# A fused attention and feed-forward kernel: a new order of all steps, with w_in's second quarter loaded ahead of batch 1's x

## The chip, the cores and the metric

The kernel runs on one core of a Trainium2 chip. The core has five instruction queues that run side by side, each strictly in its own order: TensorE (PE in the profile; its weight loads are PEld), VectorE (DVE), ScalarE (ACT), GpSimd (POOL) and SyncE (SP). SP computes nothing and issues DMAs; POOL computes and issues DMAs too. An instruction that waits for another engine holds up all that stands behind it in its queue. The metric is the device time of one execution in microseconds (us). Three runs of the kernel before took 211.12, 211.23 and 211.58 us; the median is 211.23 us.

## The reference: what is computed

There are 8 batches of 8 heads. Each head has 512 tokens and 32 states of width 64.

```python
scores = scale * x @ state.T                 # tokens read states
xread  = softmax(scores) @ state
scores2 = scale * state @ x.T                # states read tokens
sread  = softmax(scores2) @ x
y = concat([xread, sread])                   # 544 rows a batch, 8 x 64 wide
h = y @ w_in                                 # 512 -> 2048
g = maximum(h, 0) + alpha * minimum(h, 0)
out = g @ w_out                              # 2048 -> 512
```

Inputs and output are float32; the matrix work is done in float16.

## The kernel before

Nothing is scheduled by a tool at build time. The string ORDER holds 1115 short tokens, one a step, and the last loop of the kernel calls the step of each token in turn. A token is a name, its numbers (mostly batch first), sometimes an engine letter (a = ACT, v = DVE, p = POOL) and, where the step opens a PSUM bank, the number of the bank (0 to 5; one more tile of two banks, "two", is shared by scores and state projections). The place of a token fixes the place of its instructions in the queue of its engine, and so which instruction waits behind which. Waits between engines follow from the tiles.

**The attention part of a batch b.** `lx.b` (L161, POOL issues a casting DMA) loads x; three x buffers take turns, so `lx.b` must wait until the state reads `rd.(b-3)` have read the old one. `xd.b` (L291, SP) writes the transposed copy xT by a transposing DMA; batches 0 and 1 are transposed on PE instead (`xt` L299, copied out by `xo` L304). `sc.b` (L314, PE) makes the scores in the tile "two". From there two softmax chains go out. Over states: `sb` (L346, DVE), `smax` (L379, DVE), `ssh` (L384, POOL), `sexp` (L393, ACT), `ssum` (L400, L401, DVE), `snorm` (L404, DVE), `wb` (L412, DVE), whose result aT is the attention weight of every token. Over tokens: `tm` (L424, DVE), `nb` (L431 on ACT or L433 on DVE), `te` (L441, ACT), `tsum` (L451), `tn` (L457 ACT or L459 POOL), `tt` (L463, SP, a transposing DMA into e2T), then `rd` (L475, PE) and `rdo` (L486), the reads of the states. Batch 0 runs with half tiles and its own scores (`tsc`, L353), and its weights are turned on PE (`at`, `ao`).

**The feed-forward part.** xread is never made: `m.b.f` (L521, PE) multiplies the states by quarter f of w_in, `mo` (L545, L547) copies the product out, and the first layer `F.b.jc` (L570, PE, 16 blocks a batch) multiplies it by the weights aT. `N` (L623, ACT) takes the negative part, `G` (L626, DVE) builds g. In batch 0 four pairs of halves (`f`, `n`, `g`; L592, L607, L611) do the same for the first blocks. `F.8` is the block of all state reads.

The second layer of batch 0 is plain: `S.0.q.k` (L640, PE) adds two blocks of g against w_out, 8 such steps for each of 4 row quarters, `O` (L657, ACT) copies out. Batches 1 to 8 use seven products instead of eight: `U` (L707, POOL or DVE) makes sums of g, `W` (L683, POOL) sums of w_out once, `P.b.p.i.c` (L728, PE, four matmuls) are the products, `K` (L744) keeps a partial bank and `Q` (L759, L761) combines and sends out through SP. The four quarters of w_in (`wi`, L207) and of w_out (`wo`, L213) and the other states (`lst`, L201) come through POOL's DMA queue, one after another in the order of the tokens. `Z.k.n` are n dummy matmuls on bank k (L232); six more stand at the very start.

ORDER is written out in full in the file; no planner runs with the kernel, and no costs or due times are in it. What sets the work around the change is only the order of tokens on each queue, the six banks and "two", and the counts of buffers (three for x, two for xT, four for output tiles).

Of the kernel before, what the change touches and what calls it, by code (L numbers as in the profile page):

```python
# [32 lines left out]
m.2.2.5.3 mo.2.2.a.1 rdo.0.a sb.2 tn.1.1.p mo.2.2.a.0 F.1.3.1 tm.2 S.0.3.0.2 W.4.1.p F.1.0.3 N.1.0 smax.2 N.1.3 G.1.3
S.0.3.4 F.1.13.0 N.1.13 S.0.0.5 nb.2.a te.2.1 S.0.3.2 ssh.p.2 G.1.0 U.1.3.0.p F.1.7.5 N.1.7 te.2.0 G.1.7 tsum.2
S.0.3.6 S.0.3.5 S.0.3.7 F.1.14.1 N.1.14 G.1.13 S.0.3.3 G.1.14 tn.2.0.p tt.1 U.1.1.1.p U.1.2.1.p xd.3 sexp.2 S.0.0.2
m.2.3.3.5 m.4.3 mo.2.3.a.0 ssum.2.0 mo.2.3.a.1 S.0.0.0 F.1.9.1 N.1.9 mo.4.3.a G.1.9 S.0.3.1 S.0.0.6 O.0.3.a snorm.v.2
P.1.2.0.1.3 F.1.11.5 N.1.11 G.1.11 wb.2 m.3.2 mo.3.2.a S.0.0.7 F.1.10.1 N.1.10 G.1.10 S.0.0.4 O.0.0.a rd.1.2 rdo.1.a
# [775 lines left out]
```

## Time and profile before

| what | value |
|---|---|
| three runs | 211.12, 211.23, 211.58 us |
| profiled execution, its own time | 210.96 us |
| its span, first to last instruction | 209.2 us |
| PE busy | 199.0 us, 2024 matmuls |
| DVE busy | 182.0 us, 273 compute instructions and 2 memsets |
| POOL busy | 165.6 us |
| ACT busy | 150.9 us |
| granted TensorE clock | 1.000 |
| DMA | 23.71 MB, 113 GB/s in the mean |

The profiled execution stands 0.27 us below the median of the runs. A PE that is called busy is not always at its peak, since the ends of matmuls are modelled: the start times of one group and the next tell more than the busy share. POOL's spans are rough. In a timeline a row holds the start, the length, the engine, the line, the operation, the tile written and the tiles read, the shape and the count; a bracket behind it tells how long the engine stood idle and what ended it. In the chain of waits, equal neighbours are merged.

### The profile page before, as it was taken

How to read it: one execution, taken by the hardware profiler on the slowest of the kernel's cores; microseconds unless marked ns; L12 is line 12 of the kernel's file. 1: busy time of each engine (PE TensorE's matmuls, PEld its weight loads, DVE VectorE, ACT ScalarE, POOL GpSimd, SP SyncE). 2: the span in 40 equal slices, each digit the busy share in tenths (PEclk: the TensorE clock that was granted, in tenths of full speed). 3: DMA queues.
4: the chain of work that ended last, by engine and by line, in shares of the span. 5: the costliest groups of instructions: out<-in, count | busy, mean ns of one | idle time of the engine just before them, and what ended most of it. 6: DMA issues, size and time to landing. Idle time of an engine off the chain costs nothing.

```text
span 209.2 us, 5108 instructions
## 1 busy us (share of the span) xinstructions
PE 199.0 (95%) x2024; PEld 132.9 (64%) x2024; DVE 182.0 (87%) x275; ACT 150.9 (72%) x293; POOL 165.6 (79%) x105
## 2 busy tenths in 40 slices
...
GB/s 167 219 204 206 206 188 130 154 156 161 120 104 147 125 93 194 68 90 168 141 109 39 104 165 97 12 93 127 75 3 53 50 50 53 0 50 103 60 150 95
DMA packets 49992, 23.71 MB, mean 113 GB/s; under 512 B 34480, under 2 KB 49456, under 8 KB 49968
## 3 DMA queue, kind: packets, MB, share of 16 engines
...
## 4 chain that ended last, share of the span: by engine, by line
PE 61%; DMA 12%; DVE 11%; POOL 11%; issue 1%; ACT 0%; SPq 0%; POOLq 0%; DVEq 0%
PE px L728 19%; PE h L570 16%; PE pv L728 9%; POOL gsum L707 7%; DVE g L626 6%; PE py L728 6%; DMA w_in_sb<-in_moe_w_in_dram 5%; DMA st<-in_state_dram 4%; PE h L579 3%; PE o L640 2%; PE m_ps L521 2%; DMA xT<-xg 2%; DMA e2T<-e 2%; DVE oq L761 1%; DVE nb L424 1%
## 5 line engine op out<-in xcount | busy, mean ns | idle before, releaser
L626 DVE SCALAR_TENSOR_TENSOR g<-neg,oma_sb,h 128x512 f16<-128x512 f32 (+1 forms) x140 | 92.3, 707 | 7.4 <-ACT neg L623 6.8
L623 ACT ACTIVATE neg<-h 128x512 f32<-128x512 f32 (+1 forms) x140 | 75.1, 579 | 20.6 <-PE h L570 15.5
L570 PE MATMUL h<-aT,m 128*128 128x512 f16 x248 | 67.3, 379 | 0.2
L728 PEld LDWEIGHTS <-gsum 128*128 128x128 f16 x480 | 46.2, 98 | 13.0 <-issue 1.5
L728 PEld LDWEIGHTS <-g 128*128 128x128 f16 x360 | 35.1, 98 | 11.2 <-issue 0.9
L707 POOL TENSOR_TENSOR gsum<-g,g 128x1024 f16<-128x1024 f16 (+1 forms) x14 | 27.8, 1990 | 11.6 <-DVE g L626 7.2
L707 POOL TENSOR_TENSOR gsum<-gsum,g 128x1024 f16<-128x1024 f16 (+1 forms) x15 | 30.0, 2003 | 8.3 <-DVE gsum L707 7.5
L570 PEld LDWEIGHTS <-m 128*128 128x128 f16 x248 | 23.8, 98 | 16.1 <-issue 1.9
L728 PE MATMUL px<-ws,gsum 128*128 128x256 f16 x240 | 32.8, 273 | 0.0
L707 POOL TENSOR_TENSOR gsum<-g 128x1024 f16<-128x1024 f16 (+1 forms) x14 | 28.8, 2064 | 0.8 <-PE pv L728 0.8
L707 POOL TENSOR_TENSOR gsum<-g,gsum 128x1024 f16<-128x1024 f16 x12 | 25.4, 2130 | 0.2
L744 ACT COPY kept<-px 128x512 f32<-128x512 f32 (+1 forms) x20 | 11.5, 577 | 11.3 <-PE px L728 9.5
L547 ACT CAST m<-m_ps 128x512 f16<-128x512 f32 x33 | 18.0, 604 | 1.9 <-PE m_ps L521 1.7
L640 PE MATMUL o<-w_out_sb,g 128*128 128x512 f16 x64 | 17.5, 380 | 1.8 <-DVE g L626 1.0
L384 POOL TENSOR_TENSOR ts<-ts,mx 128x1024 f32<-128x1024 f32 x7 | 13.4, 1913 | 5.9 <-DVE mx L379 5.9
L728 PE MATMUL py<-w_out_sb,g 128*128 128x256 f16 x120 | 17.5, 273 | 0.1
L728 PE MATMUL px<-w_out_sb,g 128*128 128x256 f16 x120 | 16.7, 272 | 0.1
L728 PE MATMUL px<-w_out_sb,gsum 128*128 128x256 f16 x120 | 16.7, 273 | 0.0
L728 PE MATMUL pv<-ws,gsum 128*128 128x256 f16 x120 | 16.1, 273 | 0.0
L728 PE MATMUL pv<-ws,g 128*128 128x256 f16 x120 | 15.7, 273 | 0.0
L761 DVE TENSOR_TENSOR oq<-pv,kept 128x512 f32<-128x512 f32 (+1 forms) x16 | 10.4, 652 | 5.2 <-PE pv L728 4.8
L521 PE MATMUL m_ps<-w_in_sb,stT 64*32 64x512 f16 x256 | 12.6, 384 | 1.1 <-DMA w_in_sb<-in_moe_w_in_dram 0.4
...
## 6 DMA issues: line engine op xcount, KB each, us to landing
...
```

The costliest lines, as they stand in the source:

```text
L384: engine(e).tensor_tensor(blocks(cols(live["ts", b], j, S)), blocks(scored(b, j)), over_blocks(cols(live["mx", b], j, S // N)), ALU.subtract,)
L521: nc.tensor.matmul(t[N * k : N * (k + 1), :], st_head(b, h)[64 * r : 64 * r + 64, :], w_in_sb[64 * r : 64 * r + 64, c, 512 * f : 512 * (f ...
L547: copier(e)(m_tile(b, f)[:, g, :], t[g])
L570: nc.tensor.matmul(h.rearrange("p (r j s) -> p r j s", r=2, j=2), ms[b, f][:, g, 128 * j : 128 * (j + 1)], weights(b, g), start=(g == 0), ...
L579: nc.tensor.matmul(h, w_in_sb[:, c, 128 * jc : 128 * (jc + 1)], XS[:, c].rearrange("p q n b -> p (q n b)"), start=(c == 0), stop=(c == n_c ...
L623: nc.scalar.activation(neg, h, RELU, bias=0.0, scale=-1.0)
L626: nc.vector.scalar_tensor_tensor(g_tile(b, jc), negs.pop((b, jc)), oma_sb[:, jc : jc + 1], hs.pop((b, jc)), ALU.mult, ALU.add,)
L640: nc.tensor.matmul(outs[b, q], g_tile(b, jc)[:, 128 * q : 128 * (q + 1)], w_out_sb[:, jc, :], start=not begun and jc == 2 * jc2, stop=left ...
L707: engine(e).tensor_tensor(t, x(), y(), op)
L728: nc.tensor.matmul(pbanks[b, name][:, i, :], of(b, c)[:, j, 128 * i : 128 * (i + 1)], moving[:, 4 * c + j, :], start=not begun and j == 0, ...
L744: copier(e)(t, pbanks[b, "x"])
L761: nc.vector.tensor_tensor(osb, pbanks[b, name], kept[b, add], ALU.add)
```

## The change

Only ORDER differs. It has 1115 tokens before and after; no step is added or taken away, and several steps change their engine or their bank. The diff touches nearly every line of the string. The first lines of both, and later lines which hold steps that the text below names, are these:

```diff
--- before.py
+++ after.py
...
-Z.1.1 Z.2.1 stc.a cx.0.0.a stt.3 wi.0 sbd.0.a Z.4.1 cx.0.1.v xt.0.0.1.5 xo.0.0.1.a sbd.1.v xt.0.0.0.0 xo.0.0.0.v
-tsc.0.1.1 lst cx.1.0.a lx.1 sto.a cx.1.1.v tsc.0.0 Z.2.1 wi.1 smax.0.0 xt.0.1.1.4 xo.0.1.1.v xt.0.1.0.5 wo.0 tsc.1.1.0
-xo.0.1.0.a tsc.1.0 Z.2.1 m.0.0.3.4 ssh.v.0.0 sc.0.1 sexp.0.0 oma wi.2 mo.0.0.a.0 mo.0.0.a.1 Z.5.1 smax.0.1 ssum.0.0
-snorm.p.0.0 ssh.v.0.1 str.0.1 sro.0.a sc.0.0 tm.0 Z.2.1 sexp.0.1 str.1.5 Z.3.1 at.0.4 ao.0.v nb.0.v ssum.0.1
-xt.1.1.1.2 xo.1.1.1.v sro.1.a m.4.0.0.1 mo.4.0.v.0 te.0.1 te.0.0 xt.1.1.0.3 xo.1.1.0.a xt.1.0.1.4 f.0.1.0.5 mo.4.0.v.1
-m.1.0 mo.1.0.v f.0.0.0.2 n.0.1.0 snorm.p.0.1 xt.1.0.0.0 at.1.1 ao.1.v n.0.0.0 xo.1.0.1.a g.0.1.0.0 g.0.0.0.1 m.0.1.3.1
-xo.1.0.0.a sc.1 m.2.0.4.0 mo.0.1.a.1 mo.0.1.a.0 mo.2.0.a.0 g.0.0.0.0 S.0.2.0.1 mo.2.0.a.1 tm.1 sb.1 F.0.5.2 F.0.4.3
-nb.1.a wo.1 g.0.1.0.1 wi.3 f.0.1.1.4 N.0.5 G.0.5 F.0.6.0 te.1.0 smax.1 N.0.4 S.0.2.1 G.0.4 F.0.7.5 te.1.1 f.0.0.1.2
-m.0.2 N.0.6 n.0.1.1 G.0.6 g.0.1.1.1 mo.0.2.a g.0.1.1.0 wo.2 wo.3 tsum.0 S.0.1.2.3 S.0.2.2 F.0.11.0 N.0.7 G.0.7 ssh.p.1
...
-F.1.15.3 F.1.2.2 G.1.8 S.0.2.6 N.1.15 G.1.15 W.2.1.p S.0.0.3.4 N.1.2 S.0.0.1 rd.0.0 lx.3 tn.1.0.a sc.2 O.0.2.a G.1.2
...
-m.3.0.0.5 mo.3.0.a.1 lx.4 xd.4 sc.3 tm.3 P.1.2.1.1 mo.3.0.a.0 sb.3 F.2.9.4 N.2.9 G.2.9 nb.3.a F.2.11.2 F.2.10.5
...
-U.1.4.0.p P.1.3.1.0 W.4.0.p U.2.1.0.p P.1.3.0.0 m.4.1.5.1 mo.4.1.a.1 nb.4.v mo.4.1.a.0 rd.2.4 rd.3.3 P.1.4.0.1 F.2.7.1
...
-G.3.5 F.3.7.4 tn.4.0.p tt.4 N.3.7 G.3.7 P.2.3.0.0 F.3.14.0 N.3.14 F.3.3.2 N.3.3 P.2.3.0.1 lx.6 G.3.8 F.3.0.3 N.3.0
-F.4.1.4 N.4.1 P.2.3.1.0 te.5.1 G.3.14 F.4.5.5 P.2.3.1.1 Q.2.0.1.a U.2.3.0.p G.3.0 sb.5 P.2.7.1.0.0 G.3.3 N.4.5 te.5.0
...
-P.3.1.1.0 P.3.1.0.0 K.3.1.a m.5.3.2.3 sc.6 sb.6 smax.6 ssh.p.6 m.6.3.1.5 mo.6.3.a.1 P.3.6.0.1 mo.5.3.a.1 mo.6.3.a.0
...
-U.4.2.0.p P.3.7.1.0 P.3.7.1.1 K.3.4.a P.3.7.0.0 F.5.0.5 N.5.0 F.5.7.3 Q.3.1.1 F.5.4.1 N.5.7 N.5.4 tm.6 nb.6.v te.6.1
...
-nb.7.v P.4.4.1.1 P.4.3.1.0 te.7.0 G.6.0 U.5.1.0.p te.7.1 P.4.4.0.0 N.6.13 P.4.3.0.0 G.6.1 G.6.4 tsum.7 tn.7.0.a
...
-P.5.6.1.1 P.5.6.0.1 N.6.12 G.6.12 P.5.6.1.0 P.5.6.0.0 tt.7 rd.7.0 ssh.p.7 sexp.7 rdo.7.a rd.6.5 Q.5.0.0 rdo.6.a
...
+Z.1.1 Z.2.1 stc.v stt.3 cx.0.1.v Z.4.1 cx.0.0.a sbd.0.v Z.5.1 xt.0.0.1.0 xo.0.0.1.v xt.0.0.0.1 Z.2.1 sbd.1.v tsc.0.1.4
+xo.0.0.0.a tsc.0.0 sto.a wi.0 lst cx.1.0.v xt.0.1.0.5 xo.0.1.0.a Z.2.1 wi.1 cx.1.1.v xt.0.1.1.0 xo.0.1.1.a sc.0.0
+smax.0.0 Z.1.1 lx.1 tsc.1.0.3 wi.2 wo.0 tsc.1.1 ssh.v.0.0 smax.0.1 sexp.0.0 ssum.0.0 m.0.0.2.5 mo.0.0.a.1 ssh.v.0.1
+mo.0.0.a.0 str.0.1 sro.0.a str.1.0 sc.0.1 tm.0 Z.4.1 sexp.0.1 Z.5.1 snorm.p.0.0 at.0.2 ao.0.v m.0.1.3.4 f.0.1.0.1
+sro.1.a ssum.0.1 snorm.p.0.1 mo.0.1.a.1 n.0.1.0 nb.0.v te.0.0 oma mo.0.1.v.0 f.0.0.0.5 g.0.1.0.1 n.0.0.0 g.0.1.0.0
+Z.2.1 m.4.0.0.4 mo.4.0.a.1 at.1.2 ao.1.v xt.1.0.0.3 g.0.0.0.1 xt.1.1.1.1 te.0.1 xo.1.1.1.v xo.1.0.0.v g.0.0.0.0 wi.3
+tsum.0 tn.0.0.p tn.0.1.p f.0.1.1.2 xt.1.1.0.4 xo.1.1.0.v n.0.1.1 g.0.1.1.0 f.0.0.1.1 xt.1.0.1.3 xo.1.0.1.v g.0.1.1.1
+mo.4.0.a.0 n.0.0.1 F.0.4.5 N.0.4 g.0.0.1.0 F.0.6.4 N.0.6 m.0.2 m.3.0.0.3 G.0.4 g.0.0.1.1 mo.0.2.a F.0.5.2 mo.3.0.a.0
+mo.3.0.a.1 G.0.6 sc.1 tm.1 N.0.5 F.0.9.5 N.0.9 G.0.5 sb.1 nb.1.a F.0.8.1 N.0.8 G.0.8 S.0.3.1.0 te.1.0 te.1.1 S.0.3.0
...
+N.0.10 G.0.10 m.1.0 G.0.11 mo.1.0.a wo.1 lx.2 S.0.2.4 W.1.0.p wo.3 S.0.1.4 ssh.p.1 tsum.1 F.0.14.3 N.0.14 G.0.14
+F.0.12.5 N.0.12 G.0.12 S.0.2.2 S.0.1.2 m.1.2 sexp.1 m.2.0.1.3 mo.2.0.a.1 S.0.2.3 S.0.3.2 mo.1.2.a S.0.1.5 ssum.1.5
...
+m.2.2.5.3 W.2.0.p W.4.0.p S.0.2.5 G.0.13 xd.2 mo.2.2.v.1 W.2.1.p mo.2.2.a.0 S.0.2.7 F.1.4.5 S.0.3.6 mo.1.3.a tt.0
...
+F.1.2.4 N.1.2 sb.2 nb.2.a S.0.0.7.3 G.1.2 smax.2 F.1.0.1 N.1.0 te.2.1 rd.0.0 lx.3 xd.3 G.1.0 S.0.1.6 rdo.0.a S.0.1.7
...
+K.1.1.a F.2.6.0 rd.1.1 G.1.11 N.2.6 rdo.1.a G.2.6 U.1.2.1.p tn.2.0.a sc.3 F.2.3.4 tm.3 F.2.11.3 N.2.11 F.2.14.1 N.2.3
...
+G.3.2 P.2.6.1.0 P.2.2.0.0 N.3.12 G.3.12 P.2.6.0.0 nb.4.a te.4.1 te.4.0 F.3.1.2 tsum.4 N.3.1 U.2.1.1.p Q.2.0.0
...
+G.3.3 P.2.5.1.0 N.3.14 G.3.14 rd.3.3 rdo.3.a ssh.p.4 m.5.3.0.2 K.2.4.a U.2.3.1.p sc.5 rt.0.5 sb.5 P.3.1.1.1.3
+P.3.1.1.0 P.3.1.0.0 rto.0.a U.2.4.1.p mo.5.3.a.1 tm.5 P.2.7.0.1.4 U.2.4.0.p F.3.8.5 sexp.4 P.2.3.1.0 ssum.4.2 lx.6
...
+mo.5.1.a P.2.4.1.1 K.3.1.a P.2.4.1.0 P.2.3.0.0 G.3.9 G.3.11 F.4.3.5 U.3.1.0.p U.3.2.0.p P.3.2.1.1.2 smax.5 P.3.2.1.0
+Q.2.0.1.a ssh.p.5 U.3.3.1.p N.4.3 G.4.3 m.5.0.1.0 sc.6 P.2.4.0.0 tn.4.0.a mo.5.0.a.1 tm.6 P.2.4.0.1 Q.2.1.0 F.4.5.0
...
+N.4.4 F.4.11.0 P.3.6.0.0 G.4.4 P.3.6.1.0 F.4.6.5 P.3.6.1.1 sb.6 N.4.11 U.3.4.0.p P.3.6.0.1 F.4.10.2 K.3.2.a G.4.11
+N.4.6 N.4.10 P.3.7.0.0.4 tn.5.1.p P.3.5.0.0 tt.4 P.3.5.1.0 P.3.7.0.1 G.4.6 sexp.5 tn.5.0.a tt.5 F.4.7.1 nb.6.a
...
+tn.7.0.a tt.6 tn.7.1.p tt.7 Q.4.0.1.v mo.7.3.a.1 P.4.7.0.1 P.4.7.0.0 F.5.10.5 P.4.7.1.0 mo.7.3.v.0 Q.4.1.1 F.6.0.3
+N.5.10 F.5.14.2 G.5.10 N.6.0 G.6.0 N.5.14 G.5.14 F.6.1.0 N.6.1 G.6.1 P.4.4.1.1 P.4.4.0.0 P.4.4.1.0 P.4.4.0.1 rd.6.4
+rd.7.5 m.6.3.3.2 rdo.6.a m.7.1.0.4 mo.7.1.a.0 rdo.7.v rt.1.5 Q.4.1.0 P.5.1.1.0.1 U.5.3.1.p rto.1.a sb.7 mo.6.3.a.0
...
```

In words, the parts of it:

- POOL's DMA queue sent w_in quarter 0, the states, x of batch 1, w_in 1, w_out 0, w_in 2, w_out 1, w_in 3, w_out 2, w_out 3, x of batch 2; it now sends w_in 0, the states, w_in 1, x of batch 1, w_in 2, w_out 0, w_in 3, w_out 2, w_out 1, x of batch 2, w_out 3.
- Batch 0's first blocks (`f`) now stand ahead of the transposes and scores of batch 1, and batch 0's second layer begins later among its first-layer blocks.
- Copies change engines: the cast of the first states, one cast of x, one state pair, six of the eight transposed pieces and eleven copies `mo` change between ACT and DVE; `nb.4` and `nb.6` go from DVE to ACT; eight of the 16 `tn` change between ACT and POOL; some of the late `U`, `K` and `Q` change engine as well.
- The two dummy matmuls that stood at the very end now stand near the start.
- All the later steps stand at new places. `rd.3` stands behind 44 products where it stood behind 23, `lx.6` right behind it; `lx.7` follows `rd.4`.

More of the change, by code (lines that the diff above doesn't have):

```diff
@@ L33 @@
[L33 to L37, printed above, removed]
```

113 lines of the change are left out of this document (56 added, 57 removed).

## The prediction

> **What bounds the kernel now.** I read the page's busy shares and slices first, then windows of the stages, then TensorE's timeline, because PE looks full from slice 6 on and its busy share hides what it lost before.
>
> ```profile
> span 209.2 us, 5108 instructions
> PE 199.0 (95%) x2024; PEld 132.9 (64%) x2024; DVE 182.0 (87%) x275; ACT 150.9 (72%) x293; POOL 165.6 (79%) x105
> ```
>
> ```profile
> 20.00:30.00 10.00, 8.58 (x69) 3.64 (x66) 9.85 (x17) 9.54 (x17) 6.73 (x6) 1.00 1.24 206
> 30.00:100.00 70.00, 69.70 (x770) 40.68 (x762) 68.17 (x94) 64.04 (x126) 67.84 (x38) 1.00 0.83 132
> 150.00:205.00 55.00, 55.00 (x477) 44.79 (x470) 40.77 (x68) 25.01 (x53) 32.91 (x18) 1.00 0.18 59
> ```
>
> The columns after the length are PE, PEld, DVE, ACT and POOL. Up to 100 us DVE, ACT and POOL are nearly as full as PE; after 150 us PE alone is. The chain of waits gives the price of one step where its engine runs without a gap:
>
> ```profile
> 33.85 0.86 PE h L570 x4
> 57.41 4.22 POOL gsum L707 x2
> 125.83 5.26 DVE g L626 x8
> 196.13 0.87 PE px L728 x8
> ```
>
> So `F` (two matmuls) costs 0.43, `P` (four) 0.435, `S` 0.43 as well, `G` 0.66, `U` 2.1 us. With these prices I count PE's real work ahead of any step in ORDER (dummies left out). All of it is 188.6 us: 124 `F` 53.5, 32 `S` 13.8, 210 `P` 91.7, the 16 `F.8` 7.0, 32 `m` at 0.34 (26.58 to 26.93 below) 10.9, the rest (`f`, scores, transposes, reads) 11.7. A step's start less the work ahead of it I call the lag: all that PE has lost so far. The span is 188.6, plus the last lag, plus a tail of 4.1 us.
>
> ```profile
> 9.34 0.41 PE L521 MATMUL m_ps<-w_in_sb,stT 64*32 64x512 f16 x8 [0.17 <-DMA w_in_sb<-in_moe_w_in_dram]
> 13.07 0.40 PE L299 MATMUL xT_ps<-ident,xg 128*128 128x128 f16 x4 [0.45 <-DMA xg<-in_x_dram]
> ...
> 14.49 0.60 PE L592 MATMUL h<-aT,m 128*128 128x256 f16 x4
> ...
> 16.04 0.39 PE L365 MATMUL at_ps<-ident,an 128*128 128x128 f16 x4
> 16.43 0.10 PEld L521 LDWEIGHTS <-stT 64*32 64x32 f16 x5 [0.18 <-DMA w_in_sb<-in_moe_w_in_dram]
> ...
> 17.63 0.41 PE L314 MATMUL sc<-xT,stT 64*32 64x256 f16 x16
> ...
> 19.03 0.59 PE L640 MATMUL o<-w_out_sb,g 128*128 128x512 f16 x2 [0.78 <-DMA w_out_sb<-in_moe_w_out_dram]
> ...
> 20.32 0.60 PE L592 MATMUL h<-aT,m 128*128 128x256 f16 x4
> ...
> 22.05 0.60 PE L592 MATMUL h<-aT,m 128*128 128x256 f16 x4
> ...
> 26.58 0.41 PE L521 MATMUL m_ps<-w_in_sb,stT 64*32 64x512 f16 x8 [0.20 <-DMA w_in_sb<-in_moe_w_in_dram]
> 26.93 1.47 PE L640 MATMUL o<-w_out_sb,g 128*128 128x512 f16 x6
> ...
> 30.65 1.03 PE L570 MATMUL h<-aT,m 128*128 128x512 f16 x4
> ```
>
> ```profile
> 93.13 1.92 PE L728 MATMUL pv<-ws,gsum 128*128 128x256 f16 x16
> ...
> 204.26 1.04 PE L728 MATMUL pv<-ws,g 128*128 128x256 f16 x8
> ```
>
> `F.0.14` at 30.65 has 16.9 us of work ahead: lag 13.7. `P.2.7.1.0` at 93.13 has 78.0: lag 15.1. `P.8.4.0.0` at 204.26 has 187.8: lag 16.5. Five sixths of the loss falls into the first 30 us; 1.4 us come by 93 and 1.4 more by the end. The change adds no PE work, so it is worth what it does to these three terms.
>
> **The start.** POOL's queue delivers its pieces one after another: the rows above show place 1 (w_in 0) used at 9.34, place 3 (x1) at 13.07, place 4 (w_in 1) at 16.43, place 5 (w_out 0) at 19.03, place 8 (w_in 3) at 26.58, so 2.5 us a piece from place 5 on. Keeping places and changing contents, w_in 1 comes at 13.07 (3.4 earlier), x1 at 16.43 (3.4 later), w_in 2 at 19.0, w_out 0 at 21.6, w_in 3 at 24.1, w_out 2 at 26.6, w_out 1 at 29.1.
>
> What stands behind these: `m.0.1` no longer waits at 16.43, and the first blocks `f` follow `at.0` and `at.1` directly. In the old order the last two of them started at 20.32 and 22.05; now they need the second half of batch 0's weights (PE reached `at.1` at 16.04) and stand behind two transposes of x1, so about 17.0 and 17.8. Batch 1's scores pay: they stood at 17.63 and move behind `mo.0.2` to about 21, and its softmax chain ends about 1 us later on DVE. I take no PE loss for that, since `F.1` begins with 23.1 us of work ahead instead of 19.9; if that cover failed, the 1 us would show at `F.1.4`.
>
> By 26.5 us the new order has done 8 `F` and 6 `S` where the old one had 6 and 5, with equal `f` and `m`: 1.3 us gained. Then `S.0.2.2` meets w_out 1 at 29.1 with 16.7 us ahead: lag 12.4 against 13.7. Further on, `S.0.2.7` (22.7 ahead) needs w_out 3, which goes out at place 11. By pieces of 2.5 that is 34.2; but place 11 was x2 before, whose transpose SP could issue only at 36.50 (row below). That gives a lag between 11.5 and 13.8; PE's own order asks 12.6. I take 13.0, nearer to the steady pace, because w_out 3 is now issued without a pause behind x2.
>
> **DVE, ACT and POOL in the middle.** Counting the DVE work ahead of PE positions with `G` at 0.66 and the softmax steps at 1.1 to 1.2 us (a row stands below), the old order has 55.3 us of it ahead of 46 us of PE work, the new one 51.2; at 30 it is 38.1 and 36.4, at 78 85.7 and 84.1. DVE was full there, so this relief of 1.6 to 4 us lets PE keep a smaller lag; ACT falls by about 2 us likewise. Past 100 us both are equal.
>
> POOL is not relieved. Its queue and SP's, with what they wait for:
>
> ```profile
> 41.06 1.18 POOL L161 DMA_DIRECT2D xg<-in_x_dram  x1 [0.64 <-DVE g L626]
> ...
> 73.14 1.22 POOL L161 DMA_DIRECT2D xg<-in_x_dram  x1
> ...
> 89.04 0.70 POOL L459 TENSOR_SCALAR e<-e,r 128x512 f16<-128x512 f16 x1
> 89.68 1.22 POOL L161 DMA_DIRECT2D xg<-in_x_dram  x1
> 90.93 2.14 POOL L707 TENSOR_TENSOR gsum<-g 128x1024 f16<-128x1024 f16 x1
> ```
>
> ```profile
> L379 DVE TENSOR_REDUCE mx<-ts x7: 1197/1210/1222, 21.5 to 144.7; 128x32 f32<-128x1024 f32 x7
> L384 POOL TENSOR_TENSOR ts<-ts,mx x7: 1902/1912/1922, 22.8 to 146.0; 128x1024 f32<-128x1024 f32 x7
> ```
>
> ```profile
> 28.44 1.24 POOL L161 DMA_DIRECT2D xg<-in_x_dram  x1
> ```
>
> ```profile
> 36.50 1.86 SPq L291 DMA_TRANSPOSE xT<-xg  x1
> ...
> 48.28 1.97 SPq L291 DMA_TRANSPOSE xT<-xg  x1
> ...
> 79.46 1.76 SPq L291 DMA_TRANSPOSE xT<-xg  x1
> ...
> 96.94 2.85 SPq L291 DMA_TRANSPOSE xT<-xg  x1
> ...
> 144.47 1.25 SPq L463 DMA_TRANSPOSE e2T<-e  x1
> ```
>
> ```profile
> DMA to landing us min/median/max: 4.3/4.3/5.4
> ```
>
> Before, `U.2.3.0` ended at 90.93 + 2.14 = 93.07 and `P.2.7.1.0`, which reads it, began at 93.13: POOL made the lag of 15.1. In the new order `lx.3` waits for `rd.0` (29.7 ahead, lag 13, plus 0.8 to read: 43.5). From there to the end of `U.3.2.0` stand 21 `U` and one `W` at 2.1, three `ssh` at 1.9, four `lx` at 1.2, two `tn` at 0.7, in all 58.1: POOL is through at 101.6, with half a us of waits 102.1. `P.3.6.0.0` reads it with 88.0 ahead: lag 13.6 to 14.1.
>
> SP's part of the same loop: `lx.6` may start only when `rd.3` (73.0 ahead) is done; then x6 must land, SP transposes it, and `sc.6` (83.9 ahead) waits. From `lx` to the issue of `xd` the rows give 6.3 (73.14 to 79.46), 7.2 (41.06 to 48.28), 7.3 (89.68 to 96.94) and 8.1 (28.44 to 36.50), and the transposes land after 4.3 to 5.4. So `rd` to `sc` takes 0.8 + 6.3 + 4.3 = 11.4 up to 14.3 us, while the new order leaves 10.9 between them (the old left 32.1, as `rd.3` stood earlier). PE must wait 0.5 to 3.4 us. The queues are quiet there (SP holds everything behind `xd.6`), so I take the short chain with half a us more, 11.9: 1.0 us on a lag of 13.5, so 14.5.
>
> The Trainium skill ("DMA: Bandwidth & Descriptors", the section on the anatomy of one DMA) gives about 2.0 us and bytes over 436 GB/s; an estimate from it is 3.2 us for these 512 KB. By it `sc.6` would not wait and POOL's 14.1 would be the bound; the four rows above say twice that, and they decide.
>
> **Late steps.** `nb` on DVE can be held up:
>
> ```profile
> L433 DVE TENSOR_SCALAR nb<-nb x4: 159/334/1357, 13.0 to 138.3; 128x2 f32<-128x2 f32 x4
> ```
>
> ```profile
> 137.55 2.13 POOL L707 TENSOR_TENSOR gsum<-gsum,g 128x1024 f16<-128x1024 f16 x1
> ...
> 138.34 1.36 DVE L433 TENSOR_SCALAR nb<-nb 128x2 f32<-128x2 f32 x1
> ```
>
> It took 1.36 us, until POOL's sum was over, against 0.16 at best. `nb.7` stays on DVE, `nb.4` and `nb.6` leave it, worth 0.2 each at the median; under a full PE I price them at nothing (if that cover is gone, 0.4 us). The Trainium skill ("SBUF — State Buffer", the rule on the shared port pair) says the second of a DVE 2-port operation and a GpSimd one fully blocks; the row agrees. By that rule alone DVE's extra early casts could also hold POOL's descriptor writing; no run here shows that.
>
> `rd.7` now stands at 123.9 ahead, right behind `rd.6`, and its `tt.7` is the last of a chain that starts at `sc.7` (114.1). Before, `tt.7` left at 144.47 and `rd.7`, 132.2 ahead at a lag of 16.4, began at 148.6, so it had cover; now about none. I allow 0.5 us (0 to 2). The tail keeps its products and four output DMAs: no change.
>
> **The sum.** Lag 14.5 after `sc.6`, plus 0.5: 15.0, against 16.5. That is 1.5 us off the profiled execution, 210.96 to 209.46. That execution lies 0.27 below the median of the runs, so against 211.23 it is 209.7.
>
> **The rivals.**
> - The gain is larger: x6 comes in the short chain and `rd.7` is ready. For it: no wait of PE on xT shows before. Then POOL's 13.6 to 14.1 is the last bound: 208.3 to 208.8.
> - Nothing changes: the start gain goes at once because w_out 3 comes as late as x2 did (36.5, lag 13.8 as before), and the old losses of 2.7 us follow. Against it: DVE's relief. Lag 16.5: 211.2.
> - It gets slower: the x6 transfer and its transpose become the bound. At 8.1 and 5.4 the chain is 14.3, PE waits 3.4 us on 13.5, and with the 0.5 of `rd.7` the lag is 17.4: 212.1. It decides from a chain of 13.6 on (lag over 16.7). For it: outputs and transposes share the DMA engines; three of the four rows lie above 7. Against it: SP is held by `xd.6` itself.
>
> **How the numbers follow.** Chances: the forecast (208.9 to 210.6) 0.50, larger gain 0.15, nothing 0.13, slower 0.22. About 0.2% (0.4 us) is what a measurement tells from no change. Faster has the first two and a small part of the third: 0.67; same 0.11; slower 0.22. The range runs from 208.2, POOL's bound, to 211.9, inside the slow rival, and leaves out some 2 in 10.
>
> **What would show it.** `F.0` and `S.0` ahead at 27 us; a wait on w_out near 29; PE waiting at `sc.6` for the transpose of x6 (near 98) by about 1 us; the last product near 202.8. If PE waits over 3 us for x6 or e2T, or `F.1.4` starts after 37, the forecast is wrong.

## The result and the profile after

The changed kernel takes 213.15 us (median of 6 runs, 212.27 to 213.55), the kernel before 211.4 us beside it (6 runs). The ratio is 1.0076, with a 95% interval from 1.0052 to 1.0101: slower by 0.8%, where 209.7 us was forecast. The time also lies above the range that was given. Runs of one kernel spread (the kernel before took 210.6 to 213.1 us over all its runs), so a few tenths of a per cent between kernels that were timed on different chips are read from the profiles as well.

The head of the page of the changed kernel, then its windows of the three stages (columns as before: length, PE, PEld, DVE, ACT, POOL, clock):

```profile
span 211.7 us, 5091 instructions
...
PE 198.8 (94%) x2024; PEld 132.4 (63%) x2024; DVE 183.9 (87%) x280; ACT 150.1 (71%) x293; POOL 161.4 (76%) x100
```

```profile
20.00:30.00 10.00, 7.74 (x75) 3.15 (x71) 8.97 (x14) 8.70 (x18) 7.88 (x7) 1.00 1.21 174
30.00:100.00 70.00, 68.56 (x726) 40.53 (x724) 67.32 (x92) 61.68 (x120) 66.54 (x37) 1.00 0.83 128
150.00:205.00 55.00, 55.00 (x452) 43.91 (x450) 42.82 (x69) 25.76 (x52) 31.84 (x16) 1.00 0.16 54
```

PE's work is the same, its clock too. Between 20 and 30 us PE is busy for 7.74 us where it was 8.58, between 30 and 100 us for 68.56 where it was 69.70: 2.0 us of the 2.5 us that the span grew lie there. The last window is as full as before. TensorE's timeline of the changed kernel shows the places:

```profile
24.61 1.03 PE L640 MATMUL o<-w_out_sb,g 128*128 128x512 f16 x4
27.04 0.41 PE L521 MATMUL m_ps<-w_in_sb,stT 64*32 64x512 f16 x8 [1.40 <-ACT e L441]
...
29.44 1.02 PE L640 MATMUL o<-w_out_sb,g 128*128 128x512 f16 x4 [0.25 <-DMA w_out_sb<-in_moe_w_out_dram]
...
31.64 1.02 PE L640 MATMUL o<-w_out_sb,g 128*128 128x512 f16 x4 [0.31 <-DMA w_out_sb<-in_moe_w_out_dram]
...
38.17 0.38 PE L570 MATMUL h<-aT,m 128*128 128x512 f16 x1
...
58.47 0.41 PE L314 MATMUL sc<-xT,stT 64*32 64x256 f16 x16 [1.12 <-DMA xT<-xg]
...
101.60 0.41 PE L314 MATMUL sc<-xT,stT 64*32 64x256 f16 x16 [0.28 <-DMA xT<-xg]
...
132.72 0.30 PE L314 MATMUL sc<-xT,stT 64*32 64x256 f16 x8 [0.66 <-DMA xT<-xg]
...
206.51 1.04 PE L728 MATMUL pv<-ws,g 128*128 128x256 f16 x8
```

Read by the lag of the prediction (start less the work ahead). `S.0.2.0`, the second pair in the first row, starts at 25.05 with 12.56 ahead: lag 12.5, as forecast for this stage. `m.0.3` (27.04) loses 1.6 us, `S.0.2.4` (29.44) and `S.0.2.2` (31.64) together 0.9; at 31.64 the lag is 14.9. `F.1.4` starts at 38.17, past the 37 that the prediction named as its limit. `sc.3`, `sc.6` and `sc.7` (58.47, 101.60, 132.72) wait for the transposed x; counted from the end of the work ahead they lose 1.3, 0.5 and 0.85. The last row has 187.8 ahead: lag 18.7, against 16.5 before and 15.0 forecast. The list of PE's waits (us in total, how often, the longest) says the same; what it does not contain is a wait for e2T, that is, for `tt.7` at `rd.7`:

```profile
PE sc L314 <- DMA xT<-xg: 2.1, 3, 1.1
PE fill L232 <- POOL pattern L192: 1.5, 1, 1.5
PE m_ps L521 <- ACT e L441: 1.4, 1, 1.4
...
PE o L640 <- DMA w_out_sb<-in_moe_w_out_dram: 0.6, 2, 0.3
```

Why `m.0.3` waits is seen on three engines. It needs the tile "two", which batch 1's scores hold. DVE and ACT of the changed kernel:

```profile
24.22 1.23 DVE L346 STREAM_TRANSPOSE ts<-sc 128x1024 f32<-128x1024 f32 x1
```

```profile
25.54 0.69 ACT L441 ACTIVATE e<-sc,nb 128x512 f16<-128x512 f32 x1 [1.19 <-DVE ts L346]
...
26.22 0.68 ACT L441 ACTIVATE e<-sc,nb 128x512 f16<-128x512 f32 x1
```

In this trace the readers of the tile run one after another: `te.1` on ACT begins when `sb.1` on DVE has read it, and `m.0.3` when `te.1` has. The scores came at 21.67, the tile is free at 26.9.

And why w_out came late is seen on POOL:

```profile
19.08 1.36 POOL L459 TENSOR_SCALAR e<-e,r 128x512 f16<-128x512 f16 x2 [2.61 <-DVE r L451]
20.40 1.54 POOL L213 DMA_DIRECT2D w_out_sb<-in_moe_w_out_dram  x2
```

Two `tn` stand ahead of `wo.2` and `wo.1` and wait for `tsum.0`, so the two pieces go out at 20.40.

### The profile page after: what moved, and what is told of

Its sections match the earlier page's. It is cut to its first block, busy times and chain, and to the rows that moved or that the text cites. A ratio compares the mean times of both kernels' runs of the same rounds, so it can differ in the third digit from the quotient of the medians.

```text
span 211.7 us, 5091 instructions
## 1 busy us (share of the span) xinstructions
PE 198.8 (94%) x2024; PEld 132.4 (63%) x2024; DVE 183.9 (87%) x280; ACT 150.1 (71%) x293; POOL 161.4 (76%) x100
## 4 chain that ended last, share of the span: by engine, by line
PE 77%; DMA 14%; DVE 5%; POOL 1%; ACT 1%; issue 1%; DVEq 0%
PE px L728 23%; PE h L570 22%; PE pv L728 11%; DMA xT<-xg 6%; PE py L728 5%; PE o L640 5%; DMA w_out_sb<-in_moe_w_out_dram 5%; PE h L579 3%; PE m_ps L521 3%; DMA st<-in_state_dram 2%; DMA out_dram<-oq 1%; PE sr_ps L475 1%; PE sc L314 1%; DVE g L611 1%; POOL e L459 1%
## 5 line engine op out<-in xcount | busy, mean ns | idle before, releaser
L707 POOL TENSOR_TENSOR gsum<-g 128x1024 f16<-128x1024 f16 (+1 forms) x15 | 30.1, 2015 | 8.3 <-DVE g L626 4.3
L707 POOL TENSOR_TENSOR gsum<-g,g 128x1024 f16<-128x1024 f16 x13 | 27.6, 2127 | 10.9 <-DVE g L626 10.9
L728 PE MATMUL px<-ws,gsum 128*128 128x256 f16 x240 | 31.4, 273 | 0.0
L707 POOL TENSOR_TENSOR gsum<-gsum,g 128x1024 f16<-128x1024 f16 x12 | 25.6, 2135 | 0.7
L744 ACT COPY kept<-px 128x512 f32<-128x512 f32 (+1 forms) x21 | 12.2, 581 | 16.3 <-PE px L728 16.3
L547 ACT CAST m<-m_ps 128x512 f16<-128x512 f32 x33 | 18.7, 594 | 3.2 <-PE m_ps L521 3.2
L728 PE MATMUL px<-w_out_sb,g 128*128 128x256 f16 x120 | 16.4, 273 | 0.0
L728 PE MATMUL pv<-ws,gsum 128*128 128x256 f16 x120 | 16.4, 273 | 0.0
L728 PE MATMUL px<-w_out_sb,gsum 128*128 128x256 f16 x120 | 15.9, 273 | 0.0
L545 ACT CAST m<-m_ps 128x1024 f16<-128x1024 f32 x13 | 13.3, 1024 | 1.0 <-PE m_ps L521 0.9
L521 PE MATMUL m_ps<-w_in_sb,stT 64*32 64x512 f16 x256 | 11.7, 383 | 1.4 <-ACT e L441 1.4
```

The source lines that it names most:

```text
L521: nc.tensor.matmul(t[N * k : N * (k + 1), :], st_head(b, h)[64 * r : 64 * r + 64, :], w_in_sb[64 * r : 64 * r + 64, c, 512 * f : 512 * (f ...
L545: copier(e)(m_tile(b, f), t)
L547: copier(e)(m_tile(b, f)[:, g, :], t[g])
L707: engine(e).tensor_tensor(t, x(), y(), op)
L728: nc.tensor.matmul(pbanks[b, name][:, i, :], of(b, c)[:, j, 128 * i : 128 * (i + 1)], moving[:, 4 * c + j, :], start=not begun and j == 0, ...
L744: copier(e)(t, pbanks[b, "x"])
```

## Experiments

All ratios below are to the kernel before, timed on the same chip.

**The start: w_out's pieces and the tile "two".** Two edits, alone and together. `wo_early`:

```diff
-xo.1.0.0.v g.0.0.0.0 wi.3
+xo.1.0.0.v g.0.0.0.0 wi.3 wo.2 wo.1
...
-F.0.11.1 N.0.11 wo.2 G.0.7
+F.0.11.1 N.0.11 G.0.7
...
-mo.1.0.a wo.1 lx.2
+mo.1.0.a lx.2
```

`m03_late`:

```diff
-S.0.1.0.2 S.0.2.0 m.0.3 mo.0.3.a smax.1
+S.0.1.0.2 S.0.2.0 smax.1
...
-N.0.10 G.0.10 m.1.0
+N.0.10 m.0.3 mo.0.3.a G.0.10 m.1.0
```

> The changed order with w_out's third and second quarters issued right behind w_in's last, ahead of batch 0's two token norms on POOL. Theory 1 (the late issue behind the norm, which waits for a DVE reciprocal, is why these quarters land at 29.4 and 31.6): they land near 26.6 and 29.2, the two waits of PE on w_out (0.44 and 0.48 us) go, the lag at S.0.2.2 falls from 15.0 to about 14.1, and the time is 0.8 to 1.0 us under the changed kernel, +0.4% against before. Rival (the DMA engines themselves were slow at that time, whatever the issue): landings stay at 29.4 and 31.6, time unchanged, +0.8%.

> The changed order with m.0.3 and its copy three PE steps later (behind F.0.10), so that its wait of 1.57 us on batch 1's exps has other work under it. Theory 1 (w_out's second quarter, landing at 31.6, is the bound behind it): the wait goes but S.0.2.4 and S.0.2.2 wait longer for w_out by the same, lag at S.0.2.2 still near 15, time within 0.3 us of the changed kernel, +0.7 to +0.8%. Rival (the wait of m.0.3 costs its 1.57 by itself): 1.3 us faster than the changed kernel, +0.2%.

> Both edits together. Theory 1: only now all three waits go: lag at S.0.2.2 near 12.8, 2.0 to 2.3 us less than the changed kernel there; at the end 1.5 to 2.3 less, -0.2% to +0.1% against before. Rival (POOL's sums or DVE bound the middle, so that early gains are given back): the early lag falls, but the end stays within 0.5 us of the changed kernel, +0.5 to +0.8%.

`wo_early` took 212.54 us, ratio 1.0039 (1.0013 to 1.0064), `m03_late` 212.9 us, 1.0080 (1.0049 to 1.0111), both together (`wo_m03`) 212.91 us, 1.0066 (1.0034 to 1.0097). The first time is what its theory 1 gave, and its PE waits for w_out no more. The second is theory 1's in time, but not for its reason, since PE does not wait longer for w_out there. The third is the rival's. PE's timeline of `m03_late`:

```profile
25.92 0.59 PE L570 MATMUL h<-aT,m 128*128 128x512 f16 x2 [0.49 <-DVE g L626]
...
27.31 0.41 PE L521 MATMUL m_ps<-w_in_sb,stT 64*32 64x512 f16 x8
29.20 0.41 PE L521 MATMUL m_ps<-w_in_sb,stT 64*32 64x512 f16 x8 [1.48 <-ACT m L545]
```

`m.0.3` no longer waits, but `F.0.11` in front of it now waits 0.5 us for a bank that DVE frees, and `m.1.0` behind it waits 1.5 us, since the copy of `m.0.3` must leave the same tile first. The 1.6 us moved to these two places and stayed. That fits a chain of users of the tile, each as long as its readers need, and not a wrong place of `m.0.3` alone; one other place was tried, so it is not shown for every place.

The 0.8 us of `wo_early` is less clear than its ratio looks. In the profiles of `m03_late` and of five kernels below (`sc_late`, `x_early`, `x_nb7`, `after_nb7`, `x_nb7_oma`), which leave w_out's loads where the change put them, PE does not wait for w_out at all; and on top of other edits the early issue brought nothing (`wo_x`, `wo_x_nb7` below). So the 0.9 us that the changed kernel's profile shows there is not in every execution, and what the late issue costs on the mean is not settled. The waits for xT differ likewise: they add up to 2.1 us in the changed kernel's profile and 2.0 in that of `after_nb7`, but to 0.8 to 1.2 in those of `wo_early`, `m03_late`, `wo_m03` and `x1_first`, which also leave the loads of x2 to x7 in their places.

**The scores that wait for xT, taken out by moving the scores.** `sc_late` moves `sc.3`, `sc.6`, `sc.7` and their `tm` back:

```diff
-tn.2.0.a sc.3 F.2.3.4 tm.3 F.2.11.3 N.2.11 F.2.14.1 N.2.3
+tn.2.0.a F.2.3.4 F.2.11.3 N.2.11 F.2.14.1 sc.3 N.2.3
...
-m.5.0.1.0 sc.6 P.2.4.0.0
+m.5.0.1.0 P.2.4.0.0
...
-rd.5.1 snorm.v.6 m.7.0.3.4 sc.7 rdo.5.a
+rd.5.1 snorm.v.6 m.7.0.3.4 rdo.5.a
```

(`sc.6` goes behind `P.3.2.0.1`, `sc.7` behind `F.5.12`.)

> The changed order with the scores of batches 3, 6 and 7 one to two us later on PE, each behind steps that were ready. Theory 1 (PE waits there for the transposed x: 1.30, 0.47 and 0.85 us, and each wait stays in the lag to the end): 2.0 to 2.6 us less than the changed kernel, -0.4% to -0.1% against before. Rival (the softmax chains behind the scores or POOL's sums come due instead): 0 to 0.7 us less, +0.4 to +0.8%.

It took 213.45 us, ratio 1.0086 (1.0046 to 1.0126): nothing gained, against theory 1. The waits for xT are gone from its list; in their place PE's timeline shows

```profile
112.91 0.59 PE L570 MATMUL h<-aT,m 128*128 128x512 f16 x2 [0.56 <-DVE g L626]
```

and from `m.7.3` (136.15) to `P.4.7.0.1` (137.36) it takes 1.21 us where the changed kernel takes 0.69, behind an `nb.7` of 0.84 us on DVE. A later score moves its softmax chain on DVE back, towards the `G` that the next blocks need: `tm.6` starts at 104.50, where the changed kernel starts it at 102.18. That this delay is what PE pays at 112.91 is my reading; it was not tested by itself.

**The same waits, taken out from the other end.** `x_early` loads x sooner and leaves the chains in place (`sc.6` alone goes two products back):

```diff
-F.1.6.1 N.1.6 sc.2 tm.2 G.1.6 W.3.1.p tn.1.1.p tt.1
+F.1.6.1 rd.0.4 rdo.0.a N.1.6 sc.2 tm.2 G.1.6 lx.3 W.3.1.p tn.1.1.p tt.1
...
-F.1.0.1 N.1.0 te.2.1 rd.0.0 lx.3 xd.3 G.1.0 S.0.1.6 rdo.0.a S.0.1.7
+F.1.0.1 N.1.0 te.2.1 xd.3 G.1.0 S.0.1.6 S.0.1.7
...
-m.5.0.1.0 sc.6 P.2.4.0.0 tn.4.0.a mo.5.0.a.1 tm.6 P.2.4.0.1
+m.5.0.1.0 P.2.4.0.0 tn.4.0.a mo.5.0.a.1 P.2.4.0.1 sc.6 tm.6
...
-U.4.1.1.p U.4.2.1.p F.4.1.1
+U.4.1.1.p lx.7 U.4.2.1.p F.4.1.1
```

`wo_x` has the edit of `wo_early` as well.

> The changed kernel with the loop of the x buffers opened and the score chains left where they are: rd.0 goes from behind F.1.0 to behind F.1.6 (bank 4 in place of 0) and lx.3 ahead of W.3.1, lx.7 goes ahead of U.4.2.1 in POOL's queue, and sc.6 alone moves behind two more products. Theory 1 (PE's waits for xT are time lost, and what ate the gain of sc_late was that it moved the softmax chains later, in front of DVE's G): the waits of 1.3 at sc.3, 0.5 at sc.6 and 0.85 at sc.7 fall to under 0.6 together, nothing new over 0.4 appears on DVE, and the time is 211.2 to 211.9. Rival (past 60 us the order runs at the pace of DVE and POOL, so that whatever is won at a score comes back as a wait for G or U): the waits for xT are gone but waits for DVE of about the same size take their place, and the time is 212.6 to 213.3.

> x_early together with wo_early (w_out's pieces 2 and 1 issued right behind w_in 3). Theory 1: both gains add, 210.4 to 211.2, at or under the kernel before. Rival: 212.0 to 212.6, no better than wo_early alone.

`x_early` took 212.11 us, ratio 1.0048 (1.0032 to 1.0064), `wo_x` 211.97 us, 1.0044 (1.0028 to 1.0059). No wait for xT is left, and both kernels lie between the two theories. DVE, POOL and PE of `x_early` show where the rest went:

```profile
133.47 1.28 DVE L433 TENSOR_SCALAR nb<-nb 128x2 f32<-128x2 f32 x1
134.67 1.39 DVE L626 SCALAR_TENSOR_TENSOR g<-neg,oma_sb,h 128x512 f16<-128x512 f32 x2
```

```profile
132.61 2.11 POOL L707 TENSOR_TENSOR gsum<-g 128x1024 f16<-128x1024 f16 x1
```

```profile
134.94 0.92 PE L521 MATMUL m_ps<-w_in_sb,stT 64*32 64x512 f16 x12
136.12 0.40 PE L521 MATMUL m_ps<-w_in_sb,stT 64*32 64x512 f16 x4 [0.26 <-DVE g L626]
136.44 0.83 PE L728 MATMUL pv<-ws,gsum 128*128 128x256 f16 x6
```

`nb.7` scales 128x2 numbers. It holds DVE for 1.28 us, up to the moment POOL's sum ends (132.61 + 2.11 = 134.72). The `G` behind it is late by that hold-up, and `m.6.2` needs two banks that `G` must free. PE takes 1.50 us for the two `m` from `m.7.3` (134.94) to `P.4.7.0.1` (136.44). Two in a row take 0.56 elsewhere (19.90 to 20.46 in the changed kernel), so 0.9 us are lost; the first expectation below counted 1.1. This is the behaviour that the prediction quoted from the kernel before (1.36 us at 138.34) and the rule that it named there, the Trainium skill's "SBUF — State Buffer" on the shared port pair; the trace agrees again.

**The one step `nb.7`.** It goes to ACT, in `x_early` (`x_nb7`), in `wo_x` (`wo_x_nb7`), in the kernel before (`before_nb7`) and in the changed kernel (`after_nb7`), and nothing else is changed in them:

```diff
-nb.7.v
+nb.7.a
```

> x_early with one step moved to another engine: nb.7 on ACT in place of DVE. In x_early the waits for xT are gone, but nb.7, a scaling of 128x2 numbers, lasted 1.28 us on DVE beside POOL's sum, and right behind it PE lost 0.3 us at m.6.2 (for a bank that DVE's G had to free) and 0.77 at P.4.7.0.1. Theory 1 (the hold-up of DVE beside POOL delays G, and this is where the gain of x_early went): both losses at 135 us fall under 0.2 and the time is 0.7 to 1.1 us below x_early, a ratio of 0.9995 to 1.0015 to the kernel before. Rival (DVE is simply full there, with or without nb.7): waits for DVE of the same sum stay between 133 and 140 us, and the ratio stays at 1.004 to 1.005.

> The same with w_out's pieces 2 and 1 issued early as well. Theory 1: the three add, ratio 0.996 to 0.999 (what then remains at the start is the wait of 1.57 at m.0.3). Rival: 1.003 to 1.005, as wo_x.

> The kernel before with nb.7 on ACT, nothing else. There nb.7 took 1.36 us at 138.34, and behind it PE lost 0.30, 0.23 and 0.22 us between 139.7 and 141.5. Theory 1: these go, 0.4 to 0.8 us faster than before (ratio 0.996 to 0.998), and the row that the prediction showed but priced at nothing had a price in the kernel before too. Rival (the prediction's: PE is full there and DVE has slack): ratio 0.999 to 1.001.

> The changed kernel with nb.7 on ACT and nothing else, the fourth corner beside the changed kernel (1.0076), x_early (1.0048) and x_nb7 (0.9984). In the changed kernel's profile nb.7 lasted 0.62 us on DVE, since PE's wait of 0.85 at sc.7 had moved it to the end of POOL's sum, and PE lost 0.24 behind it. Theory 1 (the wait for x7 and the hold-up of nb.7 lie over each other, so that removing one shows the other): 0.2 to 0.6 us gained, ratio 1.005 to 1.007, clearly less than the 0.6% that the same edit gave on x_early. Rival (the two add): ratio 1.000 to 1.003.

| kernel | ratio to before | 95% interval |
|---|---|---|
| changed | 1.0076 | 1.0052 to 1.0101 |
| `after_nb7` | 1.0050 | 1.0025 to 1.0075 |
| `x_early` | 1.0048 | 1.0032 to 1.0064 |
| `x_nb7` | 0.9984 | 0.9963 to 1.0006 |
| `wo_x_nb7` | 0.9994 | 0.9974 to 1.0014 |
| `before_nb7` | 0.9965 | 0.9942 to 0.9988 |

`x_nb7` takes 211.48 us: against the kernel before, no loss is left that can be measured. By the ratios the step to ACT is worth 0.6% on `x_early`, 0.3% on the changed kernel and 0.35% on the kernel before (210.47 us against 211.37 in the same series of runs). The 0.6% is too much: its two ratios come from different chips, and the two times are 0.6 us apart (0.3%). PE of `x_nb7` (the second row holds `m.7.3` and `m.6.2` whole, the third begins with `P.4.7.0.1`):

```profile
37.31 0.59 PE L570 MATMUL h<-aT,m 128*128 128x512 f16 x2
...
134.39 0.94 PE L521 MATMUL m_ps<-w_in_sb,stT 64*32 64x512 f16 x16
135.27 1.05 PE L728 MATMUL pv<-ws,gsum 128*128 128x256 f16 x8
...
204.22 1.04 PE L728 MATMUL pv<-ws,g 128*128 128x256 f16 x8
```

The two `m` take 0.88 us there: 0.3 us is left of the 0.9 that `x_early` lost. From `F.1.4` (37.31) to its last row `x_nb7` takes 166.91 us and `x_early` 167.51 (37.89 to 205.40), so the 0.6 us stay to the end, and they are all that the step brings.

In the kernel before, the price had been in view. Its PE beside the row that the prediction quoted:

```profile
139.66 0.60 PE L728 MATMUL px<-w_out_sb,gsum 128*128 128x256 f16 x4
140.40 0.59 PE L570 MATMUL h<-aT,m 128*128 128x512 f16 x2
141.06 0.60 PE L728 MATMUL px<-w_out_sb,g 128*128 128x256 f16 x4
141.72 0.59 PE L570 MATMUL h<-aT,m 128*128 128x512 f16 x2
```

The steps are 0.74, 0.66 and 0.66 us apart where one takes 0.435 and the next 0.43. PE looks busy there, because the modelled length of a group (0.60) covers all or most of each gap; only the start times show 0.75 us lost. With `nb.7` on ACT the same steps start 0.43 to 0.44 apart:

```profile
140.19 0.60 PE L728 MATMUL px<-w_out_sb,gsum 128*128 128x256 f16 x4
140.62 0.59 PE L570 MATMUL h<-aT,m 128*128 128x512 f16 x2
141.05 0.60 PE L728 MATMUL px<-w_out_sb,g 128*128 128x256 f16 x4
```

In the changed kernel's profile `nb.7` took 0.62 us, `sc.7` waited 0.85 us for xT just ahead of it, and PE lost 0.1 us between `m.7.3` (136.87) and `P.4.7.0.1` (137.56). From `F.1.4` to the last row it takes 168.34 us with `nb.7` on DVE and 168.30 (37.68 to 205.98) with `nb.7` on ACT. So in these two profiles the wait for x7 hides the hold-up, as theory 1 says; the 0.3% that was measured is not seen there, and its interval overlaps that of the changed kernel.

`nb.7` stands on DVE in both kernels, so what it costs is no part of what the change did. With it on ACT in both, the change costs about as much as with it on DVE in both: `after_nb7` has 1.0050 where `before_nb7` has 0.9965. And `x_nb7`, without the waits for xT, is still behind `before_nb7`, on the same chip: 211.17 to 211.92 us against 210.11 to 210.90 in ten of its twelve runs (212.1 in the other two), 0.2% by the ratios and 0.5% by the medians; the intervals of the two ratios overlap. `before_nb7` is the fastest kernel of this study.

**The named part by itself.** `x1_first` undoes it in the changed kernel, `before_w1_first` does it alone in the kernel before:

```diff
-Z.2.1 wi.1 cx.1.1.v xt.0.1.1.0 xo.0.1.1.a sc.0.0 smax.0.0 Z.1.1 lx.1 tsc.1.0.3
+Z.2.1 lx.1 wi.1 cx.1.1.v xt.0.1.1.0 xo.0.1.1.a sc.0.0 smax.0.0 Z.1.1 tsc.1.0.3
```

```diff
-tsc.0.1.1 lst cx.1.0.a lx.1 sto.a cx.1.1.v tsc.0.0 Z.2.1 wi.1 smax.0.0
+tsc.0.1.1 lst cx.1.0.a wi.1 lx.1 sto.a cx.1.1.v tsc.0.0 Z.2.1 smax.0.0
```

> The changed kernel with only the first named part undone: lx.1 again ahead of wi.1 in POOL's queue, all else as changed. If the early arrival of w_in 1 is what the changed start lives on: m.0.1 waits for w_in until about 16.4 (3.3 us later than now), the waits at S.0.2.4 and S.0.2.2 (0.9 together) go because w_out comes no later while PE does, and the time is 214.5 to 215.5. Rival (the start is paced by the tile of two banks and by DVE, so that it makes up for the late w_in by 31 us): 213.0 to 213.6.

> The kernel before with only that part done: wi.1 ahead of lx.1, nothing else. PE's order there still asks for batch 1's x first (its first transpose waited to 13.07 for it). Theory 1: the transposes wait until about 16.4, all behind them moves by some 2 to 3 us less what DVE's lead hides, m.0.1 loses its small wait: 212.8 to 214.0, so the first named part alone harms, and the gain at the start came from the new places behind it. Rival (the loss is absorbed before w_out's pieces, which arrive at the same times): 211.2 to 211.8.

`x1_first` took 215.28 us, 1.0196 (1.0177 to 1.0215), inside the first range that was expected of it; `before_w1_first` 215.48 us, 1.0206 (1.0181 to 1.0231), more than either theory gave. The rows of the one and of the other:

```profile
16.54 0.41 PE L521 MATMUL m_ps<-w_in_sb,stT 64*32 64x512 f16 x8 [2.96 <-DMA w_in_sb<-in_moe_w_in_dram]
```

```profile
16.87 0.50 PE L299 MATMUL xT_ps<-ident,xg 128*128 128x128 f16 x4 [3.68 <-DMA xg<-in_x_dram]
```

Each order lives on its own piece coming at 13 us. By the ratios the wait of 3 us costs the changed kernel 2.5 us at the end (1.2%), and 3.2 us of added wait cost the kernel before 4.1 us (2.1%, PE's wait there was 0.45): little or nothing is absorbed behind. So the loading order can't be swapped alone: it has to fit the order of PE's steps.

**DVE at the start.** `x_nb7_oma` moves `oma`, which DVE did in 1.05 us beside POOL's `snorm`, ahead of `smax.0.1`:

```diff
-tsc.1.1 ssh.v.0.0 smax.0.1 sexp.0.0
+tsc.1.1 ssh.v.0.0 oma smax.0.1 sexp.0.0
...
-nb.0.v te.0.0 oma mo.0.1.v.0
+nb.0.v te.0.0 mo.0.1.v.0
```

> x_nb7 with oma, the one TENSOR_SCALAR on DVE (128x16 numbers), moved ahead of smax.0.1, where POOL has no work; at its place in the changed order it lasted 1.05 us beside POOL's snorm, in the kernel before 0.175. Theory 1 (what paces PE between 15 and 30 us is DVE's order and the tile of two banks): DVE is 0.8 us earlier from 15 us on, the readers of sc.1 too, the wait at m.0.3 shrinks and the ratio falls to 0.994 to 0.997. Rival (w_in, x1 and w_out set the pace up to 30 us, by their landings): ratio 0.998 to 0.9995, and the 0.8 us turns up as waits for x1 near 16 us or w_out near 29 us.

It took 211.14 us, 0.9977 (0.9956 to 0.9997), between the two theories and, within the noise, the same as `x_nb7`. `oma` of the changed kernel, then DVE of `x_nb7_oma`:

```profile
14.70 1.05 DVE L270 TENSOR_SCALAR oma_sb<-alpha_cols 128x16 f32<-128x16 f32 x1
```

```profile
9.73 0.17 DVE L270 TENSOR_SCALAR oma_sb<-alpha_cols 128x16 f32<-128x16 f32 x1
...
16.11 0.42 DVE L368 COPY aT<-at_ps 128x512 f16<-128x512 f16 x1 [0.29 <-PE at_ps L365]
...
17.63 0.76 DVE L304 COPY xT<-xT_ps 128x512 f16<-128x512 f16 x2 [0.71 <-PE xT_ps L299]
```

The instruction shrinks to 0.17 us, DVE is earlier and then idles 1.0 us for PE. So DVE's order does not set the pace at 15 us, and the wait at `m.0.3` stays as long as it was.

**All waits at once.** `rework` places the steps of `wo_x_nb7` anew by the times that each engine needs. Its diff touches nearly all lines; two lines of each (the old ones are those of the changed kernel) show the kind:

```diff
-sro.1.a ssum.0.1 snorm.p.0.1 mo.0.1.a.1 n.0.1.0 nb.0.v te.0.0 oma mo.0.1.v.0 f.0.0.0.5 g.0.1.0.1 n.0.0.0 g.0.1.0.0
-Z.2.1 m.4.0.0.4 mo.4.0.a.1 at.1.2 ao.1.v xt.1.0.0.3 g.0.0.0.1 xt.1.1.1.1 te.0.1 xo.1.1.1.v xo.1.0.0.v g.0.0.0.0 wi.3
...
+ao.0.v f.0.1.0.1 nb.0.v f.0.0.0.5 ssum.0.1 mo.0.1.a.1 wo.1 m.4.0.0.4 Z.2.1 n.0.1.0 mo.0.1.v.0 n.0.0.0 g.0.1.0.1
+g.0.1.0.0 g.0.0.0.1 snorm.p.0.1 at.1.2 mo.4.0.a.1 xt.1.0.0.3 ao.1.v xt.1.1.1.1 te.0.0 te.0.1 f.0.1.1.2 xt.1.1.0.4
...
```

> From wo_x_nb7, with the steps placed anew so that, by the engine times of the traces, PE waits less: 333 of the 1115 steps stand more than 8 places from where they stood, the loads of w_in 3, w_out 1 and w_out 3 earlier, some sums of g earlier and most sums of w_out later. If the waits that are left (1.57 at m.0.3, 0.78 at sc.1, some 1.5 in many small ones) are a matter of places alone, 208.5 to 210, below the kernel before. Rival (DVE and ACT are full up to 45 us, and what is won at one tile is lost at the next, as with m03_late): 210.3 to 211.3.

It took 223.01 us, 1.0534 (1.0487 to 1.0582), a plain miss of both theories. By its lag it is some 4 us behind `x_nb7` after 12 us of work already. The first line of its list of PE's waits names another part, and SP's timeline shows it:

```profile
PE sr_ps L475 <- DMA e2T<-e: 3.4, 3, 2.4
```

```profile
128.82 1.79 SPq L291 DMA_TRANSPOSE xT<-xg  x1
130.70 1.09 SPq L762 DMA_DIRECT2D out_dram<-oq  x1
131.88 1.27 SPq L463 DMA_TRANSPOSE e2T<-e  x1
```

`tt.5` had come to stand behind `xd.7` on SP, which waited for its x, and `rd.5` waited 2.4 us for `tt.5`. The sum that led to this order had no such queue in it. Its other losses were not followed up.

## Why the prediction was wrong

Two terms of its sum failed above all. The start was taken at a lag of 13.0 and came to 15.0, because the step that gave it "no PE loss" overlooked the tile "two"; and of the scores only `sc.6` was priced (1.0 us, measured 0.5), while `sc.3` and `sc.7`, put at nothing, lost 2.15 us. Point by point, by its own steps:

- **The start** was right up to 25 us: lag 12.5. It failed in the sentence "I take no PE loss for that, since `F.1` begins with 23.1 us of work ahead". The softmax chain of batch 1 has more readers than `F.1`: it holds the tile "two", and `m.0.3` stood behind that tile. Cost 1.6 us; PE idles there for 1.35 to 1.40 us in every profile that keeps `m.0.3` at that place, and moving it by three steps (`m03_late`) only moved the wait. The prediction asked for the consumer of the chain's result and not for the next user of its buffer. With this wait the start brought no gain: even where w_out comes in time, the lag at `F.1.4` is 14.2 (`x_nb7`, 37.31), and the kernel before had 13.7 at `F.0.14`.
- **w_out** was dated by its place in the queue, with pieces of 2.5 us. Two `tn` that wait for `tsum.0` stand ahead of its issue on POOL, so the two pieces left at 20.40. They were forecast for 26.6 and 29.1; they landed at 29.40 and 31.60 in the changed kernel's profile, which shows 0.9 us of waits, and at 27.1 to 27.4 and 30.0 to 30.9 in those of `after_nb7`, `sc_late`, `x_early` and `x_nb7`, which show none. Its mean is not settled.
- **DVE's relief** of 1.6 to 4 us brought nothing that can be seen. In the window from 30 to 100 us DVE is about as full as before (67.3 of 70 us against 68.2).
- **POOL's bound** was misread. "POOL made the lag of 15.1" rested on a sum that ended at 93.07 and a product that began at 93.13. The row ahead of it in the kernel before is

```profile
92.61 0.60 PE L728 MATMUL px<-w_out_sb,gsum 128*128 128x256 f16 x4
```

  and this product (four matmuls, 0.435) ends at 93.05: PE did not wait. The lag grows in small steps, not at one bound. `x_nb7`, which has none of the waits for xT, has a lag of 14.2 at `F.1.4` (37.31) and 16.4 at its last row (204.22), so 2.2 us of growth; the changed kernel has 1.1 beside its three waits, and the forecast allowed 0.5. So of the 2.65 us of those waits, only 1.4 come back when they and `nb.7`'s hold-up are gone (168.34 against 166.91 us from `F.1.4` on): part of them only covered small losses that then show elsewhere.
- **`sc.6`** went as forecast: the short chain, 11.4 us from `rd.3` (90.16) to `sc.6` (101.60), and 0.5 us of waiting where 1.0 was taken. But it is one of three. `lx.3` and `lx.7` had moved as well, and their scores were not followed: POOL issues `lx.3` at 45.74 and SP the transpose at 54.08, 8.3 us later, and `lx.7` goes out only at 121.21 with `sc.7` due at 132. These two were put at nothing and cost 1.3 and 0.85 us in this profile. POOL's timeline of the changed kernel, then SP's:

```profile
45.74 1.23 POOL L161 DMA_DIRECT2D xg<-in_x_dram  x1
...
90.92 1.19 POOL L161 DMA_DIRECT2D xg<-in_x_dram  x1 [0.15 <-issue]
...
121.21 1.23 POOL L161 DMA_DIRECT2D xg<-in_x_dram  x1
```

```profile
54.08 2.89 SPq L291 DMA_TRANSPOSE xT<-xg  x1
```

- **`nb` beside POOL**, "under a full PE I price them at nothing": this failed for both kernels. The row with 1.36 us cost the kernel before 0.75 us in its profile and 0.35% in the measurement. In the changed kernel `nb.7` stays on DVE; it costs PE 0.1 us there by the profile, and 0.6 us more (0.3%) once the waits for xT are gone. As it stood on DVE before too, this step did not make the change slower.
- **`rd.7`** at 0.5 us: nothing, no wait for e2T.

By the lag, 15.0 was forecast and 18.7 came. The start took 2.0 more than the 13.0 that was forecast for `S.0.2.7` (it stands at 15.0), `sc.3` and `sc.7` 2.15, `sc.6` and `rd.7` came 1.0 cheaper, and 0.6 is spread. (The price of 0.34 for an `m` is too high where two stand in a row, which take 0.56 together; that shifts the lags of both kernels by some tenths of a us.) The rival "slower" had the right kind of mechanism, the transfer and transpose of an x, but at x6; it was x3 and x7 that cost more, and that its 212.1 us lies nearest to the measured time is in part luck, since it had nothing of the start's 2.0. What is shown by taking it away: without the waits for xT and with `nb.7` on ACT the changed order is level with the kernel before (0.9984), and against the kernel before with the same step on ACT it is still 0.2 to 0.5% behind. Where this rest lies stays open; no edit removed the wait for the tile "two". What also stays open is the mean price of w_out's late issue and of the waits for xT, which differ between executions.
